# First batch's attention and first weight conversions in a fixed order, with the states requested ahead of the input

## The chip, the cores and the metric

The kernel runs on one core of one Trainium2 chip. The metric is device time in microseconds (us) of one execution; shorter is better. The profile is one execution recorded by the hardware profiler. Engines are named as in the profile: PE is TensorE (PEld its weight loads), DVE is VectorE, ACT is ScalarE, POOL is GpSimd, SP is SyncE, which only issues transfers here. A "q" behind an engine's name is that engine issuing a transfer.

## The reference

Three stages follow one another: an attention of each batch against a small state and back, a product MoE layer, and an eight-expert layer with one expert for each token.

```python
scores = scale * np.matmul(x, state.transpose(0, 1, 3, 2))      # x (8,8,512,64), state (8,8,32,64)
a = np.exp(scores - scores.max(-1, keepdims=True))
a /= a.sum(-1, keepdims=True) + 1e-09
xread = np.matmul(a, state)
# sread: the same with the roles of x and state exchanged
x = concat([xread, sread]) as (4608, 512)
x = (x @ w_a) * (x @ w_b) @ w_out                               # w_a, w_b (512,1536), w_out (1536,512)
# then per token: e = argmax(x @ w_gate), gate * sigmoid * (relu(x @ w1[e]) @ w2[e])
```

## The kernel before, in words

Phase 1 goes batch by batch (`main(b)`, b = 0 to 7). The attention of a batch gives a matrix A. The state, multiplied into the weights w_a and w_b, gives a matrix M for each of six groups of 256 columns (`mprep`). A times M (`s1`, twelve steps f, two products each on PE, line 511) gives the two factors; ACT and DVE multiply them and split the product into a high and a low part (`product` and `split`, lines 490 to 498 and 248 to 250). The split product is multiplied by the split w_out (`s2`, line 524). So M of group g needs w_a and w_b of group g, and the first `s2` needs the first two blocks of w_out.

**Conversions.** The weights are not used as they lie in memory. `converter` is a generator over 18 items, in the order (0,a), (0,b), (1,a), (1,b), w_out 0, (2,a), (2,b), w_out 1 and so on. Each item is loaded in two requests on SP's queue into one of two buffers (the tiles y and yT, not otherwise used so early), goes through two passes on ACT (line 184 writes cr, line 185 writes cx) and three on DVE (line 186 a shift of cx, line 196 a merge that is the last reader of the loaded data, line 199 an add of cr). Items of w_out have one more pass on ACT (line 209, wo_h) and one on DVE (line 210, wo_l). The load of item i + 2 is requested once line 196 of item i has read the buffer.

**The first batch.** The attention of batch 0 is not hidden behind another batch's work. A list, `CFG["pro"]`, gives the order in which its units are written: "stt" turns the state (with a copy of it on POOL first, line 240, since the turned state needs two copies side by side), "x0" to "x3" turn the input in quarters (line 309, copies to SBUF at lines 315 and 317), "sc" the scores (324, copies 336 and 337), "af0", "af1" turn the scores and make the exponentials (346, 351, 352, 355), "an" the sums and the division (377 to 382, one half on DVE, the other on POOL), "ab0", "ab1" turn A back and split it (445, 249, 250), "m" is `mprep` of group 0 (480, 249, 250) and "c" is one conversion. Five conversions stand in this list. The other 13 are placed in `main(0)` by `CFG["conv"]`, a count for each of 24 slots: slot 0 comes behind `s1` of f = 0, and for f from 1 on slot 2f - 1 comes behind `s1` of f and slot 2f behind the `s2` of f - 1 that follows it. The `mprep` of groups 1 to 5 stands in slots 1, 5, 9, 13 and 17 of batch 0.

**What sets the order.** The source is not the order of execution. A scheduler takes the instructions of each engine by their place in the source and its own estimate of when their inputs are ready, so that an instruction may be placed ahead of one that stands before it in the source. Each engine then executes its instructions strictly in the order given.

Of the kernel before, what the change touches and what calls it, by code (L numbers as in the profile page):

```python
# [36 lines left out]
SCALE = 0.125  # L37
BYPE = 2
CFG = {
    "pro": ["c", "stt", "x0", "x3", "x1", "x2", "sc", "c", "af0", "af1", "c", "an", "c", "ab0", "ab1", "m", "c"],  # L40
    "conv": [0, 1, 0, 1, 1, 0, 1, 1, 1, 0, 1, 1, 1, 0, 1, 1, 1, 0, 0, 1, 0, 0, 0, 0],
    "at0": [10, 14, 10, 12, 15, 15, 15, 18, 18, 20, 21, 23, 23, 23],
    "at": [6, 7, 9, 10, 11, 13, 14, 17, 18, 15, 19, 21, 22, 23],
    "gate": [1, 2, 3, 5, 6, 7, 9, 10, 11, 17],
# [7 lines left out]
class Phase1:  # L52
# [30 lines left out]
    def run(self, ctx, moe2):  # L83
# [35 lines left out]
        self.conv = self.converter(order)  # L119
        self.att = u = self.attention(0)  # L120
        conv = lambda n: [next(self.conv, None) for _ in range(n)]
        units = {"m": lambda: self.mprep(0, 0), "c": lambda: conv(1)}
        for n, v in u.items():
            units.update({n + str(i): w for i, w in enumerate(v)} if isinstance(v, list) else {n: v})
        for n in CFG["pro"]:
            units[n]()
        self.banks = cycle([(self.ps_x, "aux")])

        for b in range(self.nb):
# [17 lines left out]
    def converter(self, order):  # L147

        nc = self.nc
        V = nc.vector
        n = 1024
        raws = {}

        def load(i):  # L160
            if i >= len(order):
                return
            it = order[i]
            raw = raws[i] = self.craw[i % 2]
            for k in range(2):
                to = raw[:, n * k : n * k + n]
                if isinstance(it, int):
                    f = 2 * it + k
                    nc.sync.dma_start(out=to, in_=self.w_out[P * f : P * f + P, :])
                else:  # L170
                    g, ab = it
                    src = (self.w_a, self.w_b)[ab][2 * P * k : 2 * P * k + 2 * P, 512 * g : 512 * g + 512]
                    nc.sync.dma_start(
                        out=to.rearrange("p (a b) -> p a b", a=2), in_=src.rearrange("(j p) f -> p j f", p=P)
                    )

        def step(i):
            raw = raws.pop(i)
            it = order[i]
            w = raw.rearrange("p (n two) -> p n two", two=2)  # L180
            lo, hi = w[:, :, 0].bitcast(U32), w[:, :, 1]
            r = self.pc.tile([P, n], U16, tag="cr", name="cr")
            x = self.pc.tile([P, n], I32, tag="cx", name="cx")
            nc.scalar.activation(out=r, in_=lo, func=AF.Copy, scale=2.0**-29)
            nc.scalar.activation(out=x.bitcast(F32), in_=hi.bitcast(F32), func=AF.Copy, scale=2.0**-112)
            V.tensor_scalar(out=x, in0=x, scalar1=3, scalar2=None, op0=ALU.logical_shift_left)
            if isinstance(it, int):
                to, v = x, lambda t: t
                half = x.bitcast(U16).rearrange("p (n two) -> p n two", two=2)[:, :, 0]
            else:  # L190
                g, ab = it
                v = lambda t: t.rearrange("p (j f) -> p j f", j=4)
                to = self.wab[:, ab, :, 256 * g : 256 * g + 256].bitcast(I32)
                half = self.wab.bitcast(U16)[:, ab, :, 512 * g : 512 * g + 512]
                half = half.rearrange("p j (f two) -> p j f two", two=2)[:, :, :, 0]
            V.scalar_tensor_tensor(
                out=to, in0=v(hi), scalar=-(1 << 31), in1=v(x), op0=ALU.bitwise_and, op1=ALU.bitwise_or
            )
            V.tensor_tensor(out=half, in0=half, in1=v(r), op=ALU.add)
            return x.bitcast(F32)  # L200

        for i in range(2):
            load(i)
        for i in range(len(order)):
            v = step(i)
            load(i + 2)
            if isinstance(order[i], int):
                h, l = (t[:, 2 * order[i] : 2 * order[i] + 2, :].rearrange("p f n -> p (f n)") for t in (self.wo_h, self.wo_l))
                nc.scalar.activation(out=h, in_=v, func=AF.Copy)  # L209
                V.tensor_tensor(out=l, in0=v, in1=h.bitcast(F32), op=ALU.subtract)  # L210
            yield
# [10 lines left out]
    def load_x(self, b):  # L222
# [2 lines left out]
        st = self.p2.tile([P, 2, 1 if turned else 2, D], F32, tag="st", name=f"st_{b}")  # L225
        srcs = self.state[b].rearrange("(j q) n d -> q j n d", q=2)
        for q in range(2):
            (nc.scalar if b == 0 else nc.sync).dma_start(out=st[:, q, 0, :], in_=srcs[q])
        if turned:
            xin = self.px.tile([P, 4, 16, 32], F32, tag="xin", name=f"xin_{b}")  # L230
            src = self.x[b].rearrange("(j k) (o i c) (a e) -> k a j i c o e", k=2, i=32, c=4, e=32)
# [4 lines left out]
                        in_=src[g // 2, g % 2, j],  # L236
                    )
            self.at.setdefault(b, {}).update(xin=xin)
        else:
            nc.gpsimd.tensor_copy(out=st[:, :, 1, :], in_=st[:, :, 0, :])  # L240
        t = self.p1.tile([P, H, 4 * D], F32, tag="x", name=f"x_{b}")
        src = self.x[b].rearrange("h (p c) d -> p h (c d)", c=4)
# [13 lines left out]
    def attention(self, b):  # L256
# [116 lines left out]
        def anorm():  # L373
# [3 lines left out]
                nc.vector.tensor_reduce(out=sm[:, g, :], in_=d["A"][:, g, :], axis=AX.X, op=ALU.add)  # L377
            nc.vector.tensor_scalar(out=sm, in0=sm, scalar1=1e-9, scalar2=None, op0=ALU.add)
            nc.vector.reciprocal(out=sm, in_=sm)
            for hf, e in enumerate((nc.vector, nc.gpsimd)):  # L380
                g = slice(16 * hf, 16 * hf + 16)
                e.tensor_tensor(
                    out=d["A"][:, g, :], in0=d["A"][:, g, :], in1=sm[:, g, :].to_broadcast([P, 16, 32]), op=ALU.mult
# [163 lines left out]
    def main(self, b):  # L547
# [25 lines left out]
                put(h, x)  # L573
        if b == 0:
            for h in range(24):
                put(h, *[lambda: next(self.conv, None)] * CFG["conv"][h])
        sl = self.slots(prog, 24)
        ys = None
        gts = {}
# [14 lines left out]
    def main_sr(self):  # L594
# [48 lines left out]
            pass  # L643
        self.acc = ys
        self.evac(self.nb)

    def gate(self, b, T):
        nc, p1, p2 = self.nc, self.p1, self.p2
# [1146 lines left out]
```

## Time and profile before

| | us |
|---|---|
| median of 3 runs (lowest to highest) | 1206.18 (1206.01 to 1207.05) |
| time of the profiled execution | 1205.72 |
| its span, first to last instruction | 1204.1 |
| first main product (`s1` of batch 0, line 511) starts | 36.85 |
| PE busy over the span | 1141.3 (95%) |
| DVE busy over the span | 628.6 (52%) |
| ACT busy over the span | 437.9 (36%) |
| mean granted PE clock, share of full | 0.975 |

The span is the time from the first to the last instruction; the profiled execution took 1.6 us more than its span. Busy shares are means over stages with different limits, so the change is read from the stretch in which it lies.

### The profile page before, as it was taken

What the parts mean: (1) busy time and instruction counts of PE and PEld (TensorE: products, weight loads), DVE (VectorE), ACT (ScalarE), POOL (GpSimd) and SP (SyncE); (2) the same over time, 40 slices, a digit from 0 to 9 for tenths busy, and PEclk for the clock granted to TensorE, in tenths of its full rate; (3) what the DMA queues carried; (4) which work ended last, traced back from release to release, by engine and by line L of the source; (5) the groups of instructions that cost most, each with busy time, mean ns of one, the idle gap of its engine ahead of it and who ended that gap; (6) DMA issues with size and microseconds to landing.
All of it is one profiled execution on the core that took longest, in us unless ns stands there. A gap on an engine that the chain in (4) does not pass through costs nothing. (4 is left out here: it accounts for less than half of the span.)

```text
span 1204.1 us, 19174 instructions
## 1 busy us (share of the span) xinstructions
PE 1141.3 (95%) x7076; PEld 906.3 (75%) x7076; DVE 628.6 (52%) x1078; ACT 437.9 (36%) x720; POOL 178.3 (15%) x282
## 2 busy tenths in 40 slices
PE   3898999999999999999999999789999999999994
PEld 2665767777777677677677789678888998888983
DVE  5889545465464364554643354842443444454462
ACT  4666424333333333333442244431321323242341
POOL 1100002001001020020010101002233123332121
PEclk7899999999999999999999999898999999999997
DMA  6563320302203003010000008539272162635610
GB/s 200 179 226 105 71 38 36 70 4 72 36 1 97 11 36 71 1 52 20 1 36 2 36 1 203 103 108 206 81 198 71 37 164 75 171 89 156 164 33 21
DMA packets 97453, 98.79 MB, mean 82 GB/s; under 512 B 58556, under 2 KB 69853, under 8 KB 97309
## 3 DMA queue, kind: packets, MB, share of 16 engines
q1 hardware_dynamic: 87508, 71.53, 23.3%
q0 software_dynamic: 9536, 25.41, 7.0%
q8 instruction: 74, 1.21, 0.4%
q14 instruction: 71, 0.57, 0.2%
q10 hardware_dynamic: 264, 0.07, 0.0%
HBM read 76.75 MB, written 21.02 MB: 81 GB/s over the span
## 5 line engine op out<-in xcount | busy, mean ns | idle before, releaser
L979 PEld LDWEIGHTS ps_h<-yT,w 128*128 128x128 f32 x1536 | 191.4, 191 | 12.2 <-issue 6.4
L979 PE MATMUL ps_h<-yT,w 128*128 128x256 f32 x1536 | 193.6, 283 | 6.1 <-issue 6.0
L1000 PE MATMUL ps_o<-w,hT 128*128 (+1 forms) x768 | 190.1, 396 | 2.4 <-DVE hT L940 2.4
L524 PE MATMUL ps_y<-wo_h,gh 128*128 128x512 f32 x408 | 165.9, 411 | 2.0 <-ACT wo_h L209 2.0
L1000 PEld LDWEIGHTS ps_o<-w,hT 128*128 128x128 f32 x768 | 139.8, 188 | 32.4 <-issue 3.0
L524 PE MATMUL ps_y<-wo_l,gh 128*128 128x512 f32 x408 | 161.5, 396 | 0.5 <-DVE wo_l L210 0.5
L524 PE MATMUL ps_y<-wo_h,gl 128*128 128x512 f32 x408 | 161.0, 395 | 0.0
L496 DVE TENSOR_TENSOR a<-a,ps_ab 128x512 f32<-128x512 f32 x96 | 65.6, 684 | 156.0 <-PE ps_ab L511 150.7
L511 PE MATMUL ps_ab<-Ah,Mh 128*128 128x512 f32 x384 | 128.3, 415 | 6.0 <-ACT Mh L249 6.0
L511 PE MATMUL ps_ab<-Al,Mh 128*128 128x512 f32 x384 | 121.6, 398 | 0.0
L511 PE MATMUL ps_ab<-Ah,Ml 128*128 128x512 f32 x384 | 120.7, 396 | 0.0
L511 PEld LDWEIGHTS ps_ab<-Ah,Mh 128*128 128x128 f32 x384 | 67.7, 191 | 58.4 <-issue 25.1
L934 ACT ACTIVATE hT<-ps_h 128x512 fp32r<-128x512 f32 x64 | 38.0, 594 | 197.5 <-PE ps_h L979 189.9
L495 ACT ACTIVATE a<-ps_ab 128x512 f32<-128x512 f32 x96 | 57.3, 597 | 118.9 <-PE ps_ab L511 118.9
L940 DVE SCALAR_TENSOR_TENSOR hT<-ps_h,hT 128x512 fp32r<-128x512 f32 x64 | 44.0, 688 | 106.0 <-ACT hT L934 106.0
L524 PEld LDWEIGHTS ps_y<-wo_h,gh 128*128 128x128 f32 x408 | 76.7, 189 | 26.3 <-issue 7.1
L249 ACT ACTIVATE gh<-a 128x512 fp32r<-128x512 f32 (+1 forms) x108 | 65.4, 605 | 83.8 <-DVE a L496 83.5
L250 DVE TENSOR_TENSOR gl<-a,gh 128x512 fp32r<-128x512 f32 (+1 forms) x108 | 71.3, 660 | 41.0 <-ACT gh L249 40.3
L960 POOL DMA_INDIRECT out<-yT,gt x37 | 46.6, 1259 | 301.9 <-DVE yT L950 224.6
L524 PEld LDWEIGHTS ps_y<-wo_h,gl 128*128 128x128 f32 x408 | 76.7, 188 | 18.4 <-DVE gl L250 0.2
L524 PEld LDWEIGHTS ps_y<-wo_l,gh 128*128 128x128 f32 x408 | 77.0, 189 | 15.6 <-DVE wo_l L210 1.0
L250 DVE TENSOR_TENSOR Ml<-ps_m,Mh 128x512 fp32r<-128x512 f32 x96 | 61.8, 686 | 48.3 <-ACT Mh L249 48.2
(245 smaller groups left out, 1398.0 us busy)
## 6 DMA issues: line engine op xcount, KB each, us to landing
raw<-in_moe_w SPq DMA_DIRECT2D x32, 512.0 KB, 10.2
raw<-in_moe_w SPq DMA_DIRECT2D x8, 2048.0 KB, 8.5
x<-in_x SPq DMA_DIRECT2D x7, 1024.0 KB
xin<-in_x SPq DMA_DIRECT2D x96, 64.0 KB
y<-in_moe_w_a SPq DMA_DIRECT2D x8, 512.0 KB
yT<-in_moe_w_b SPq DMA_DIRECT2D x8, 512.0 KB
y<-ysort POOLq DMA_DIRECT2D x28, 128.0 KB, 5.8
y<-in_moe_w_out SPq DMA_DIRECT2D x6, 512.0 KB
```

Of the source, the lines that this page charges most:

```text
L249: self.nc.scalar.activation(out=hi, in_=src, func=AF.Copy)
L250: self.nc.vector.tensor_tensor(out=lo, in0=src, in1=hi.bitcast(F32), op=ALU.subtract)
L495: nc.scalar.activation(out=a[:, 0:n], in_=pa[:, 0:n], func=AF.Copy)
L496: nc.vector.tensor_tensor(out=a[:, 0:n], in0=a[:, 0:n], in1=pb[:, 0:n], op=ALU.mult)
L511: nc.tensor.matmul(out=ps, lhsT=m[:, ab, q, c0 : c0 + P], rhs=r[:, q, :], start=i == 0, stop=i == 5)
L524: nc.tensor.matmul(out=y, lhsT=l[:, sl], rhs=r[:, f, :], start=f == 0 and i == 0, stop=f == NFC - 1 and i == 2)
L934: return e.activation(out=self.hT[:, j % 2, :, 0, :], in_=self.ps_h[j % 2].rearrange("p (f n) -> p f n", f=2), func=AF.Relu)
L940: return e.scalar_tensor_tensor(out=l, in0=self.ps_h[j % 2].rearrange("p (f n) -> p f n", f=2), scalar=0.0, in1=h.bitcast(F32), op0=ALU.ma ...
L960: return e.indirect_dma_start(out=self.out, out_offset=bass.IndirectOffsetOnAxis(ap=to[0:rows].bitcast(U32), axis=0), in_=self.ob[t][0:row ...
L979: m = e.matmul(out=self.ps_h[j % 2][:, G * (f % 2) : G * (f % 2) + G], lhsT=self.w1[:, wh, x : x + P], rhs=self.yT[:, c, yh, :], start=k == 0,
L1000: m = e.matmul(out=self.ps_o[2 * (k % 2) + t], lhsT=self.hT[:, j % 2, f, hh, P * t : P * t + P], rhs=self.w2c(slot, wh, 2 * j + f), start= ...
```

## The change

In the list of the first batch, the attention's units stand first, in their natural order; the first conversion follows the scores; three conversions remain in the list instead of five, and the two others move into `main(0)`, in slots 0 and 1 (item (1,b) and w_out 0). Items (2,a), (2,b) and w_out 1 go from slots 1, 3 and 4 to slots 3, 4 and 5; from slot 6 on the slots hold the same items as before. A conversion is now two units: "ca", its two ACT passes, with cx (line 185 before) written ahead of cr, and "cd", its three DVE passes, the next load and the passes for w_out. `pin` adds an order without any wait between successive instructions of the list on PE, ACT and DVE, so that the scheduler keeps the source's order among them. A unit "warm" runs one tiny ACT instruction at the start. The states of batch 0 are requested twice, on SP's queue ahead of the input and on ACT's queue, each into one of the two places, in place of the copy on POOL. Both halves of the first batch's division are on DVE.

```diff
-    "pro": ["c", "stt", "x0", "x3", "x1", "x2", "sc", "c", "af0", "af1", "c", "an", "c", "ab0", "ab1", "m", "c"],
-    "conv": [0, 1, 0, 1, 1, 0, 1, 1, 1, 0, 1, 1, 1, 0, 1, 1, 1, 0, 0, 1, 0, 0, 0, 0],
+    "pro": "warm stt x0 x1 x2 x3 sc ca af0 af1 cd ca an cd ab0 ab1 m ca cd".split(),
+    "conv": [1, 1, 0, 1, 1, 1, 1, 1, 1, 0, 1, 1, 1, 0, 1, 1, 1, 0, 0, 1, 0, 0, 0, 0],
...
+            "warm": lambda: nc.scalar.activation(out=warm, in_=self.ones[:, 0:1], func=AF.Copy),
...
+        at = self.mark()
         for n in CFG["pro"]:
             units[n]()
+        self.pin(at, nc.tensor, nc.scalar, nc.vector)
...
+            nc.scalar.activation(out=x.bitcast(F32), in_=hi.bitcast(F32), func=AF.Copy, scale=2.0**-112)
             nc.scalar.activation(out=r, in_=lo, func=AF.Copy, scale=2.0**-29)
-            nc.scalar.activation(out=x.bitcast(F32), in_=hi.bitcast(F32), func=AF.Copy, scale=2.0**-112)
+            yield
...
-            (nc.scalar if b == 0 else nc.sync).dma_start(out=st[:, q, 0, :], in_=srcs[q])
+            nc.sync.dma_start(out=st[:, q, 0, :], in_=srcs[q])
+            if b == 0:
+                nc.scalar.dma_start(out=st[:, q, 1, :], in_=srcs[q])
...
-        else:
+        elif b:
             nc.gpsimd.tensor_copy(out=st[:, :, 1, :], in_=st[:, :, 0, :])
...
-            for hf, e in enumerate((nc.vector, nc.gpsimd)):
+            for hf, e in enumerate((nc.vector, nc.gpsimd if b else nc.vector)):
...
-                put(h, *[lambda: next(self.conv, None)] * CFG["conv"][h])
+                put(h, *[lambda: next(self.conv, None)] * (2 * CFG["conv"][h]))
...
+    def mark(self):
+        return len(self.nc.cur_bb.bb.instructions)
+
+    def pin(self, at, *engines):
+
+        last = {}
+        for i in self.nc.cur_bb.bb.instructions[at:]:
+            if i.engine not in [e.engine for e in engines]:
+                continue
+            if i.engine in last:
+                self.tc.add_manual_dep(
+                    i,
+                    last[i.engine].name,
+                    mybir.DependencyInfo(mybir.DependencyClass.NoSync, mybir.DependencyReason.DATA),
+                    reason="in the order of the source",
+                )
+            last[i.engine] = i
```

## Rows read from the trace of the kernel before

**Rows 1.** Stretches: start:end, length, busy us of each engine, PEclk, DMA share, GB/s.
```profile
0.00:36.80 36.80, 14.37 (x84) 7.99 (x84) 23.00 (x31) 17.14 (x21) 8.57 (x26) 0.69 0.63 206
...
36.85:59.00 22.15, 22.13 (x111) 16.19 (x110) 19.04 (x25) 15.00 (x23) 0.00 (x0) 0.89 0.49 153
59.00:125.00 66.00, 57.24 (x382) 40.97 (x383) 61.09 (x79) 42.73 (x59) 2.41 (x2) 0.97 0.47 157
...
155.00:808.00 653.00, 646.90 (x4009) 489.08 (x4008) 335.65 (x702) 234.74 (x431) 63.45 (x124) 0.99 0.19 47
```
**Rows 2.** Waits of PE, whole execution: us in total, times, longest.
```profile
PE ps_ab L445 <- DVE A L382: 7.0, 1, 7.0
PE ps_ab L511 <- ACT Mh L249: 6.0, 4, 2.2
...
PE ps_ab L445 <- POOL A L382: 1.4, 1, 1.4
```
**Rows 3.** Timeline of the first 17 us: start, us, what, [idle before <-releaser].
```profile
0.95 2.00 SPq L245 DMA_DIRECT2D x<-in_x  x4
0.95 1.77 ACTq L228 DMA_DIRECT2D st<-in_state  x2
...
3.86 0.44 PE L309 MATMUL ps_xt<-ident,x 128*128 128x128 f32 x1 [3.86 <-DMA x<-in_x]
...
7.37 0.28 POOL L240 COPY st<-st 128x128 f32<-128x128 f32 x1 [5.76 <-DMA st<-in_state]
...
8.19 3.13 PE L309 MATMUL ps_xt<-ident,x 128*128 128x128 f32 x15
...
9.93 1.28 ACT L184 ACT_TABLE_LOAD   x1 [9.93 <-DMA y<-in_moe_w_a]
...
13.89 2.43 PE L324 MATMUL ps_s<-xT,stT 64*32 64x256 f32 x32 [2.57 <-ACT xT L315]
...
16.63 0.67 DVE L337 COPY sc<-ps_s 128x512 f32<-128x512 f32 x1
```
**Rows 4.** Groups of DVE, first 36.8 us: busy us, mean ns, idle before.
```profile
L199 DVE TENSOR_TENSOR wab<-wab,cr 128x1024 uint16<-128x1024 uint16 x4 | 5.4, 1359 | 0.0
L186 DVE TENSOR_SCALAR cx<-cx 128x1024 int32<-128x1024 int32 x5 | 3.5, 700 | 2.2 <-ACT cx L185 2.2
L196 DVE SCALAR_TENSOR_TENSOR wab<-y,cx 128x1024 int32<-128x1024 int32 x2 | 2.5, 1234 | 0.0
...
L351 DVE TENSOR_REDUCE mx<-ps_af 128x16 f32<-128x512 f32 x2 | 1.4, 696 | 0.7 <-PE ps_af L346 0.7
...
L387 DVE TENSOR_REDUCE m<-sc 128x2 f32<-128x1024 f32 x1 | 1.2, 1237 | 0.0
L382 DVE TENSOR_TENSOR A<-A,sm 128x512 f32<-128x512 f32 x1 | 0.7, 726 | 0.0
```
**Rows 5.** Timeline of PE's `mprep` and the conversions' third load.
```profile
15.40 0.90 SPq L173 DMA_DIRECT2D y<-in_moe_w_a  x2
...
20.72 1.14 ACT L184 ACTIVATE cr<-y 128x1024 uint16<-128x1024 uint32 x1 [3.73 <-DMA y<-in_moe_w_a]
...
22.46 1.96 PE L480 MATMUL ps_m<-wab,stT 64*32 64x512 f32 x16 [3.45 <-DVE wab L199]
```
**Rows 6.** Groups of ACT, first 36.8 us.
```profile
L249 ACT ACTIVATE Mh<-ps_m 128x512 fp32r<-128x512 f32 x2 | 1.1, 586 | 0.0
```
**Rows 7.** Timeline behind the start of `s1`: PE at two clocks, DVE's longest wait.
```profile
39.58 1.06 PE L511 MATMUL ps_ab<-Ah,Mh 128*128 128x512 f32 x2
...
42.18 0.69 DVE L496 TENSOR_TENSOR a<-a,ps_ab 128x512 f32<-128x512 f32 x1 [2.46 <-ACT sc L390]
...
43.27 0.62 PE L511 MATMUL ps_ab<-Ah,Mh 128*128 128x512 f32 x2
```
**Rows 8.** Waits of DVE, 36.8 to 120 us: us in total, times, longest.
```profile
DVE cx L186 <- ACT cx L185: 2.5, 3, 1.2
```
**Rows 9.** A stretch ahead of `s1`, columns as in the first group.
```profile
24.00:36.00 12.00, 3.57 (x18) 1.61 (x10) 10.57 (x16) 6.61 (x9) 3.64 (x1) 0.50 0.60 206
```

More of the change, by code (lines that the diff above doesn't have):

```diff
@@ L121, in run @@
         conv = lambda n: [next(self.conv, None) for _ in range(n)]
-        units = {"m": lambda: self.mprep(0, 0), "c": lambda: conv(1)}
+        warm = self.cpool.tile([P, 1], F32, name="warm")
+        units = {
+            "m": lambda: self.mprep(0, 0),
+            "ca": lambda: conv(1),
+            "cd": lambda: conv(1),
+            "warm": lambda: nc.scalar.activation(out=warm, in_=self.ones[:, 0:1], func=AF.Copy),
+        }
         for n, v in u.items():
             units.update({n + str(i): w for i, w in enumerate(v)} if isinstance(v, list) else {n: v})
+        at = self.mark()
         for n in CFG["pro"]:
             units[n]()
+        self.pin(at, nc.tensor, nc.scalar, nc.vector)
         self.banks = cycle([(self.ps_x, "aux")])
@@ L204, in converter @@
         for i in range(len(order)):
-            v = step(i)
+            v = yield from step(i)
             load(i + 2)
```

## The prediction

> **What bounds the kernel now.** I read the stretches first, then PE's waits, then the first 45 us instruction by instruction, since every edit lies there. Outside the first batch PE sets the time: from 155 to 808 us it is busy for 646.9 of 653 us [rows 1]. What is gained or lost ahead of that is therefore passed on to the end; I found nothing later that is tied to a fixed time.
>
> In the first 36.8 us PE is busy for 14.37 us and DVE for 23.00 [rows 1]: a chain through DMA, ACT and DVE sets the time. The reader is to see in the rows where the attention stands behind a conversion. The state lands at 7.37, and PE had stood since one early transpose at 3.86 [rows 3]. The scores are late because ACT loads its table at 9.93 and runs conversion passes ahead of the turned input (PE waits 2.57) [rows 3]. A is late because DVE weaves four conversions into the softmax: PE waits 7.0 us for the division on DVE and 1.4 more for the half on POOL [rows 2]. The first `s1` starts at 36.85.
>
> Behind that the bound is not PE alone. From 59 to 125 us PE is idle for 66 - 57.24 = 8.76 us while DVE is busy for 61.09 of 66; PE's largest wait there is for M [rows 1, 2], which ends a chain of conversions. So an early `s1` is worth no more than the lead that DVE gets on its conversions. That is the quantity to work out.
>
> **State, table, input.** The copy on POOL goes (it is 0.28 us behind the landing [rows 3]). SP now issues two state requests before the input. The two on ACT's queue took 1.77 us, so I delay the input, and the loads behind it, by 1.77 [rows 3]. When the state lands is not shown for the new order. Lower end: the first input quarter landed 3.86 - 0.95 = 2.91 us after its issue began; the second state request begins half of 1.77 after 0.95, so 1.8 + 2.9 = 4.7. Upper end: 7.3 as now, if its small pieces again wait among those of the input. I take 5.5, nearer to the lower end, since the input's requests now start only when all state requests are out. ACT's two requests end at 2.72 as now; the table load of 1.28 follows them and ends near 4.1. ACT has nothing else until the first turned quarter after 6, so it costs nothing; without this cover it would cost 1.28. The tiny activation behind it goes with it.
>
> Then, in source order: 18 transposes at 3.13/15 = 0.21 us [rows 3] run from 5.5 to 9.3. The last input quarter landed before 8.19 (the 15 transposes ran without a wait), so before 9.96 with the delay; I take 9.5 for the end of the transposes. The last turned quarter leaves through DVE (0.69, like the copy at 16.63), a quarter of the scores follows (2.43/4 = 0.6), and the score copies (0.67): 9.5 + 0.7 + 0.6 + 0.7 = 11.5. Before, this point was 17.3 [rows 3]: **5.8 us earlier**.
>
> **Softmax, two conversions, M.** From here on DVE's order is the source's. Four transposes at twice 0.21, since the clock was at half in this part [rows 9], with their start: 1.0. Two maxima and two subtractions at 0.70: 2.8. Conversion 0: 0.70 + 1.23 + 1.36 = 3.3. The sums twice 0.70, two small steps taken at 0.6, and two halves of the division at 0.73, where before one was on POOL: 3.5. Conversion 1: 3.3 [rows 4]. `mprep` 1.96 [rows 5] and the first Mh 0.59 [rows 6]. The split of A and its transposes fit beside `mprep` and conversion 1. Sum: 1.0 + 2.8 + 3.3 + 3.5 + 3.3 + 2.0 + 0.6 = 16.5. Successive DVE spans overlap: the groups of the first stretch add up to some 25.7 us, of which 23.00 is union over 31 instructions [rows 1], or 0.09 for each; 14 of them give back 1.2. So `s1` starts at 11.5 + 15.3 = 26.8, **10 us earlier**. The ACT passes of conversion 0 need their load, which had landed by 9.93; with 1.77 more it comes at 11.7, just as the scores are out, and ACT has cx ready long before DVE asks at 15.3.
>
> **What of the 10 us is DVE's.** At 36.85 DVE before had done four conversions, the shift of the fifth and the maximum of the second softmax (line 387). In the new order it ends the low part of M at 28.1 (26.8 plus the second Mh and two overlapped subtractions) with two conversions done. It lacks two conversions 6.6, the shift 0.7 and line 387 1.2, and has done half a division more, 0.7 [rows 4]: 7.8, less 0.09 for each of nine overlaps, 7.0. It is level at 35.1: a **lead of 1.7 us**, not 10. The moved conversions bring their loads along. A buffer asked for at 15.40 was used at 20.72 [rows 5], 5.3 us. The load of item 3 is requested after line 196 of conversion 1, near 22.5, and lands near 27.8, in time; that of item 4 after conversion 2, near 30.5, and lands near 35.8. ACT, which works in order, may hold M's copies behind it; DVE has conversion 3 and two products meanwhile. SP has nothing else queued behind them.
>
> On top comes DVE's wait of 2.46 for the first product, ending at 42.18 [rows 7]: with `s1` ten us earlier this product is there when DVE comes. That gives 1.7 + 2.4 = 4.1. Writing cx ahead of cr lets line 186 start one ACT pass sooner; it waited 2.5 in three places from 36.8 to 120 [rows 8], which I bound between 0 and 2.3. Against it stands PE's clock: `s1` starts at half clock as before, and I expect some idle time of PE until w_out 0 is ready, and so another stretch at half clock. I set these two off against each other.
>
> The sum: **4.0 us**. The profiled execution took 1205.72, which gives 1201.7; the median of the runs is 0.5 higher, so I forecast **1202.2**. Its own range is a gain of 2.5 to 6: 1200.2 to 1203.7.
>
> **Rivals.**
>
> *PE's lead is kept* (0.13). If the scheduler fills DVE and ACT well, PE keeps most of its 10 us; at most the 8.76 us of PE's idle time from 59 to 125 shrinks too. For it: ACT is busy for only 42.73 of those 66 us. Against it: DVE is at 93% there [rows 1]. I give it a gain of 6 to 8.8: 1197.4 to 1200.2, in the middle 1198.8.
>
> *The state comes no earlier* (0.23). It lands at 7.3, and the transposes then end 1.8 later; the lead on DVE falls from 1.7 to zero and only the wait of 2.4 is gained, which a little less overlap takes below what can be told. The time would be 1206.2 - 2.2 = 1204.0. For it: the state was asked for at 0.95 already and was the last thing that PE waited for [rows 3]. Against it: it was asked for together with the input then. The Trainium skill (Trainium Kernel Development and Optimization, Key Constraints) says that requests from several queues run on the same DMA engines and interleave, and that issuing from more than one saves only issue time. By that rule the order on the queues buys no landing time except through what is requested earlier, and the input pays its 1.77; the result would be this rival's 1204.0 and not 1202.2. The landing at 7.37 beside the input agrees with interleaving. I call the bound for telling a change of this kernel from none 0.2%, 2.4 us; this rival stands at its edge, and I count it as no change.
>
> *PE falls back to half clock inside the batch, slower* (0.09). Place: between the second `s1` and the first `s2`. Two `s1` steps end near 34; w_out 0, now behind the batch's start, lands near 35.8 and takes an ACT pass, three DVE passes and line 209 before `s2` can start near 41. Seven idle us may take the clock down; with the stretch at 0.50 before `s1` in view [rows 9], that is what idle time did. A pair of products took 1.06 at half clock and 0.62 behind it [rows 7], 0.22 for each. It decides once more than 4.0/0.22 = 18 products of 512 columns run at half clock on PE's path; 36 (two `s2` and an `s1`) cost 7.9, which gives 1206.2 + 3.9 = 1210.1. For it: PE had no idle time from 36.85 to 59 [rows 1], so there each lost us counts. Against it: the clock was back at 43.27 after the first `s1` [rows 7], and DVE's pace hides a part.
>
> **How the numbers follow.** Forecast 0.55, the three rivals 0.13, 0.23 and 0.09. Faster by over 0.2% (below 1203.8): 0.55 + 0.13 = 0.68. Within 0.2%: 0.23. Slower by over 0.2%: 0.09. The range leaves out the far end of the first rival and the last rival: 1198.0 to 1206.5, where the upper end is a lead that is lost wholly.
>
> **What would show each step.** State: POOL's copy gone, the first stt transpose between 4.7 and 7.3. Input: the last turned quarter near 9.5. Scores: the copies end near 11.5. No wait of PE for POOL; `s1` starts near 26.8. Lead of DVE: the products that wait for the second group's M some 4 us earlier than before, and the end of the first batch by as much. The prediction is wrong if the state lands as late as now, if the scheduler weaves later work into the list despite the fixed order, or if DVE or ACT finds new waits for loads after `s1`'s start. It is also wrong if a later stage gives the gain back.

## The result, and the profile after

The changed kernel took 1213.99 us (median of 5 runs, 1211.98 to 1217.94) beside 1207.05 for the kernel before on the same chip: a ratio of 1.0058 [1.0044, 1.0073], about 7 us slower. Forecast were 1202.2 and a range up to 1206.5. The profiled execution took 1213.99, its span 1212.3.

The stretches come first, with the columns of [rows 1]; the last two are new.

```profile
0.00:36.80 36.80, 18.60 (x103) 11.85 (x104) 21.80 (x32) 17.01 (x25) 4.54 (x24) 0.77 0.51 162
36.85:59.00 22.15, 15.01 (x70) 10.51 (x69) 19.84 (x23) 14.24 (x18) 0.00 (x0) 0.77 0.63 205
59.00:125.00 66.00, 57.67 (x378) 40.76 (x378) 59.41 (x77) 42.04 (x56) 1.24 (x2) 0.95 0.50 165
155.00:808.00 653.00, 647.17 (x4006) 488.22 (x4006) 335.71 (x702) 234.23 (x430) 63.70 (x124) 0.99 0.19 48
...
36.00:48.00 12.00, 4.86 (x27) 2.29 (x26) 11.02 (x13) 7.71 (x11) 0.00 (x0) 0.68 0.71 241
```

PE does 4.23 us more in the first 36.8 us (18.60 against 14.37), so the attention is earlier. But between 36.85 and 125 it stands for 7.14 + 8.33 = 15.47 us, where it stood for 0.02 + 8.76 = 8.78 before: 6.69 more. That leaves a net loss of 2.5 us. DVE is busy for 21.80 us in the first stretch instead of 23.00, though it now has half a division more to do. The stretch from 155 to 808 is as before. The places where PE stands are in the view of its waits (whole execution, columns as in [rows 2]):

```profile
PE ps_y L535 <- ACT wo_h L218: 9.5, 3, 3.6
PE ps_ab L456 <- DVE A L393: 9.0, 2, 8.7
PE ps_m L491 <- DVE wab L208: 5.4, 2, 3.5
PE ps_st L276 <- DMA st<-in_state: 5.1, 2, 3.9
PE ps_ab L522 <- ACT Mh L260: 2.1, 2, 1.4
```

The wait for `Mh` fell from 6.0 to 2.1 us, and the one for POOL is gone. The wait for the division is still there, for both halves on DVE now. A wait of 9.5 us for `wo_h` took their place; before it was 2.0:

```profile
PE ps_y L524 <- ACT wo_h L209: 2.0, 2, 1.8
```

PE's own timeline shows where each lies (start, us, what, [idle before <-releaser]):

```profile
3.92 0.45 PE L276 MATMUL ps_st<-ident,st 128*128 128x128 f32 x1 [3.92 <-DMA st<-in_state]
5.53 0.47 PE L276 MATMUL ps_st<-ident,st 128*128 128x128 f32 x1 [1.16 <-DMA st<-in_state]
5.80 1.91 PE L320 MATMUL ps_xt<-ident,x 128*128 128x128 f32 x8
8.78 2.27 PE L320 MATMUL ps_xt<-ident,x 128*128 128x128 f32 x8 [1.06 <-DMA x<-in_x]
10.98 2.47 PE L335 MATMUL ps_s<-xT,stT 64*32 64x256 f32 x32
...
30.66 1.65 PE L522 MATMUL ps_ab<-Ah,Mh 128*128 128x512 f32 x3 [0.72 <-ACT Mh L260]
...
41.30 1.96 PE L491 MATMUL ps_m<-wab,stT 64*32 64x512 f32 x16 [3.54 <-DVE wab L208]
46.87 2.07 PE L535 MATMUL ps_y<-wo_h,gh 128*128 128x512 f32 x4 [3.60 <-ACT wo_h L218]
...
78.44 2.08 PE L535 MATMUL ps_y<-wo_h,gh 128*128 128x512 f32 x4 [2.47 <-ACT wo_h L218]
...
97.17 1.20 PE L535 MATMUL ps_y<-wo_h,gh 128*128 128x512 f32 x4 [3.44 <-ACT wo_h L218]
```

The first `s1` starts at 30.66 instead of 36.85. PE runs two of them, then stands for 3.54 us for the second group's M and, behind that, for 3.60 for w_out 0. In the stretch 36 to 48 the granted clock is 0.68 (before it was 0.77 there, with `s1` beginning at half clock), and the four products at 46.87 take 2.07 us: half clock again, after idle time. On DVE (timeline, same columns) the reader is to see what stands ahead of the first conversion, and when each merge (line 205) comes:

```profile
13.53 0.69 DVE L348 COPY sc<-ps_s 128x512 f32<-128x512 f32 x1 [1.75 <-PE ps_s L335]
14.33 1.22 DVE L398 TENSOR_REDUCE m<-sc 128x2 f32<-128x1024 f32 x1
...
18.83 1.23 DVE L205 SCALAR_TENSOR_TENSOR wab<-y,cx 128x1024 int32<-128x1024 int32 x1
...
25.16 1.23 DVE L205 SCALAR_TENSOR_TENSOR wab<-yT,cx 128x1024 int32<-128x1024 int32 x1
...
32.90 1.23 DVE L205 SCALAR_TENSOR_TENSOR wab<-y,cx 128x1024 int32<-128x1024 int32 x1
...
38.17 1.22 DVE L205 SCALAR_TENSOR_TENSOR wab<-yT,cx 128x1024 int32<-128x1024 int32 x1
...
42.45 1.23 DVE L205 SCALAR_TENSOR_TENSOR cx<-y,cx 128x1024 int32<-128x1024 int32 x1
```

The same on DVE before, where the merge is line 196:

```profile
13.38 0.69 DVE L186 TENSOR_SCALAR cx<-cx 128x1024 int32<-128x1024 int32 x1 [1.91 <-ACT cx L185]
14.11 1.23 DVE L196 SCALAR_TENSOR_TENSOR wab<-y,cx 128x1024 int32<-128x1024 int32 x1
...
19.23 1.21 DVE L196 SCALAR_TENSOR_TENSOR wab<-yT,cx 128x1024 int32<-128x1024 int32 x1
...
25.69 1.24 DVE L196 SCALAR_TENSOR_TENSOR wab<-y,cx 128x1024 int32<-128x1024 int32 x1
...
29.56 1.21 DVE L196 SCALAR_TENSOR_TENSOR wab<-yT,cx 128x1024 int32<-128x1024 int32 x1
...
37.11 1.22 DVE L196 SCALAR_TENSOR_TENSOR cx<-y,cx 128x1024 int32<-128x1024 int32 x1
```

The first five merges end at 20.1, 26.4, 34.1, 39.4 and 43.7 us. Before, they ended at 15.3, 20.4, 26.9, 30.8 and 38.3: items 0 to 4 are 4.7, 6.0, 7.2, 8.6 and 5.4 later. The next load is issued behind each merge, so SP's requests moved too: 20.12 for the third, where [rows 5] have 15.40.

The first batch's end is read from the first copy-out of its output. Before and after (timeline of ACT):

```profile
130.53 0.60 ACT L533 ACTIVATE y<-ps_y 128x512 f32<-128x512 f32 x1 [2.38 <-PE ps_y L524]
```
```profile
134.54 0.60 ACT L544 ACTIVATE y<-ps_y 128x512 f32<-128x512 f32 x1 [2.38 <-PE ps_y L535]
```

It is 4.0 us later. From there to about 740 us the lag stays between 3.9 and 3.6 us, then grows to 8.2 at the end of this execution. So two things are to be explained: 4 us in the first 125, and some more in the expert stage.

### The profile page after: what moved, and what is told of

It is laid out like the page before. It is cut to its first block, busy times and chain, and to the rows that moved or that the text cites. A ratio compares the mean times of both kernels' runs of the same rounds, so it can differ in the third digit from the quotient of the medians.

```text
span 1212.3 us, 19185 instructions
## 1 busy us (share of the span) xinstructions
PE 1144.1 (94%) x7076; PEld 907.8 (75%) x7076; DVE 630.3 (52%) x1079; ACT 438.4 (36%) x721; POOL 173.3 (14%) x280
## 5 line engine op out<-in xcount | busy, mean ns | idle before, releaser
L1008 PEld LDWEIGHTS ps_h<-yT,w 128*128 128x128 f32 x1536 | 194.1, 192 | 12.2 <-issue 6.4
L1008 PE MATMUL ps_h<-yT,w 128*128 128x256 f32 x1536 | 196.6, 284 | 6.1 <-issue 6.0
L522 PEld LDWEIGHTS ps_ab<-Ah,Mh 128*128 128x128 f32 x384 | 68.5, 193 | 54.1 <-issue 25.1
L506 ACT ACTIVATE a<-ps_ab 128x512 f32<-128x512 f32 x96 | 57.3, 597 | 119.2 <-PE ps_ab L522 119.2
```

The costliest lines, as they stand in the source:

```text
L506: nc.scalar.activation(out=a[:, 0:n], in_=pa[:, 0:n], func=AF.Copy)
L522: nc.tensor.matmul(out=ps, lhsT=m[:, ab, q, c0 : c0 + P], rhs=r[:, q, :], start=i == 0, stop=i == 5)
L1008: m = e.matmul(out=self.ps_h[j % 2][:, G * (f % 2) : G * (f % 2) + G], lhsT=self.w1[:, wh, x : x + P], rhs=self.yT[:, c, yh, :], start=k == 0,
```

## The experiments

After the result my theory was this (A in the forecasts below). The order without waits holds conversions back behind the attention on DVE; the chain of conversions, with its loads, is what PE's output steps wait for; so an earlier `s1` buys nothing and late conversions cost. Its rivals: the two conversions that left the list are missed (B); the state requests delay the input; the tiny ACT instruction or its tile costs something (C); PE's own order (two `s1`, then the output step at the head of its queue while w_out 0 is not ready) makes the wait (D).

Every run in one table. `s1` and `s2` are the starts of the first of each; "first batch" is the start of the first copy-out less 130.53; all these come from one profiled execution of each kernel. "Whole" is the median less that of the kernel before on the same chip. The ratio goes by all runs and not by the medians, so where the difference is small its sign can be another (e1). The profiled execution need not be near the median: e1's took 1201.45 us (median 1206.02), g2's 1216.39 (median 1210.47). None of these kernels leaves out part of the computation.

| kernel | s1 | s2 | first batch | whole | ratio [95%] |
|---|---|---|---|---|---|
| before | 36.85 | 45.73 | 0 | | |
| changed | 30.66 | 46.87 | +4.0 | +6.9 | 1.0058 [1.0044, 1.0073] |
| e1_no_pin | 32.49 | 45.40 | -3.0 | -0.5 | 1.0006 [0.9989, 1.0022] |
| e2_five | 30.74 | 46.12 | +0.2 | +1.7 | 1.0021 [1.0004, 1.0037] |
| e3_warm_only | 36.04 | 45.00 | -0.6 | +1.7 | 1.0012 [0.9999, 1.0025] |
| e4_state_only | 38.35 | 46.33 | +0.8 | +2.1 | 1.0019 [1.0002, 1.0036] |
| f1_pin_pe_act | 28.57 | 45.37 | +1.8 | +6.1 | 1.0043 [1.0028, 1.0058] |
| f2_no_tile | 29.50 | 46.94 | +4.4 | +6.3 | 1.0048 [1.0029, 1.0066] |
| f3_no_pin_no_tile | 32.33 | 45.24 | -3.7 | -1.4 | 0.9976 [0.9960, 0.9992] |
| f4_swap | 29.93 | 51.70 | +1.2 | +5.3 | 1.0038 [1.0018, 1.0058] |
| g1_dve_free_swap | 29.02 | 50.49 | +0.1 | +0.8 | 1.0003 [0.9986, 1.0021] |
| g2_pin_pe | 34.36 | 44.34 | +2.7 | +3.6 | 1.0037 [1.0021, 1.0052] |
| g3_early | 33.06 | 45.74 | -0.5 | +1.1 | 1.0014 [0.9994, 1.0035] |
| g4_best_old_state | 30.24 | 44.74 | -4.0 | -3.4 | 0.9972 [0.9958, 0.9985] |
| h1_output_first | 32.59 | 45.24 | -3.8 | -0.3 | 1.0001 [0.9986, 1.0015] |
| h2_before_swap | 36.31 | 48.78 | +0.2 | +1.7 | 1.0010 [0.9995, 1.0025] |
| h3_tile_only | 36.60 | 44.86 | +1.3 | +0.9 | 1.0004 [0.9993, 1.0016] |
| h4_best_five | 30.29 | 40.87 | -1.4 | -1.9 | 0.9983 [0.9967, 0.9999] |

h3 sets the scale: one unused tile more moves the first batch by 1.3 us, so a difference of that size in one trace is not put down to an edit. Two other pairs that differ in the tile alone, the changed kernel and f2, e1 and f3, agree within 0.4 and 0.7.

### One part at a time

**e1_no_pin**: the changed kernel without the order among the list's instructions.

```diff
-        self.pin(at, nc.tensor, nc.scalar, nc.vector)
```

> The changed kernel without the fixed order; everything else stays. Theory A (the conversions come too late: the fixed order keeps DVE idle in the attention and delays conversion 0 by 4.7 us): the scheduler weaves the conversions between the attention's units again, line 196's counterpart for item 0 ends some 3 us earlier than in the changed kernel, and the time falls by 2 to 4 us, to 1209 to 1212. Theory B (it is the moving of two conversions into the batch, whatever the order in the list): the first output step still waits for w_out 0, the time stays within 1.5 us of the changed kernel. Theory C (the loss of some 4 us behind 760 us has a cause of its own, the addresses moved by the tiny tile): unchanged there.

The first batch ends 7.0 us sooner than in the changed kernel and 3.0 sooner than before. DVE's timeline:

```profile
13.94 0.69 DVE L194 TENSOR_SCALAR cx<-cx 128x1024 int32<-128x1024 int32 x1 [4.40 <-ACT cx L191]
14.55 0.68 DVE L327 COPY xT<-ps_xt 128x512 f32<-128x512 f32 x1
15.15 1.21 DVE L204 SCALAR_TENSOR_TENSOR wab<-y,cx 128x1024 int32<-128x1024 int32 x1
...
26.23 1.19 DVE L204 SCALAR_TENSOR_TENSOR wab<-y,cx 128x1024 int32<-128x1024 int32 x1
```

The first conversion is back where DVE has nothing else, ahead of the score copies, and the third merge ends at 27.4, not 34.1. This is against rival B, that the two moved conversions alone cost the time: they are still moved here. `s1` starts 1.8 us later than in the changed kernel, and it doesn't matter. The whole time fell by more than forecast, to that of the kernel before and not below; the part behind the first batch is taken up below.

**e2_five**: the order kept, but five conversions in the list, as before, and the slots of before.

```diff
-    "pro": "warm stt x0 x1 x2 x3 sc ca af0 af1 cd ca an cd ab0 ab1 m ca cd".split(),
+    "pro": "warm stt x0 x1 x2 x3 sc ca af0 af1 cd ca an cd ca ab0 ab1 m cd ca cd ca cd".split(),
-    "conv": [1, 1, 0, 1, 1, 1, 1, 1, 1, 0, 1, 1, 1, 0, 1, 1, 1, 0, 0, 1, 0, 0, 0, 0],
+    "conv": [0, 1, 0, 1, 1, 0, 1, 1, 1, 0, 1, 1, 1, 0, 1, 1, 1, 0, 0, 1, 0, 0, 0, 0],
```

> The changed kernel with five conversions in the list again (in the same fixed order, the two behind M's group 0) and the slots of before. Theory B (moved conversions): the first output step no longer waits long for w_out 0 and the first batch ends within 1 us of before; time 1207 to 1210. Theory A (the fixed order delays all conversions): the first product starts 3 to 6 us later than in the changed kernel because ScalarE and VectorE work on conversions ahead of it, and nothing is won: still 3 to 5 us behind before at the end of the first batch.

+0.2 instead of +4.0. With the order in force, moving two conversions behind the list costs 3.8 us. This is what rival B said, and a miss for theory A. Three of e2's merges, for items 0, 2 and 4:

```profile
18.90 1.22 DVE L205 SCALAR_TENSOR_TENSOR wab<-y,cx 128x1024 int32<-128x1024 int32 x1
...
32.64 1.23 DVE L205 SCALAR_TENSOR_TENSOR wab<-y,cx 128x1024 int32<-128x1024 int32 x1
...
41.10 1.23 DVE L205 SCALAR_TENSOR_TENSOR cx<-y,cx 128x1024 int32<-128x1024 int32 x1
```

The first three merges end at 20.1, 26.4 and 33.9 us, as late as in the changed kernel; items 3 and 4 end at 37.6 and 42.3, 1.8 and 1.4 sooner, and PE's wait for `wo_h` falls from 9.5 to 2.5 us. So a late first conversion is not enough for the loss, and by e1 neither is the move of two: it takes both.

**e3_warm_only** and **e4_state_only**: the kernel before with the tiny ACT instruction alone, and with the new state requests alone.

```diff
...
+        warm = self.cpool.tile([P, 1], F32, name="warm")
...
+            "warm": lambda: nc.scalar.activation(out=warm, in_=self.ones[:, 0:1], func=AF.Copy),
...
```
```diff
-            (nc.scalar if b == 0 else nc.sync).dma_start(out=st[:, q, 0, :], in_=srcs[q])
+            nc.sync.dma_start(out=st[:, q, 0, :], in_=srcs[q])
+            if b == 0:
+                nc.scalar.dma_start(out=st[:, q, 1, :], in_=srcs[q])
...
-        else:
+        elif b:
             nc.gpsimd.tensor_copy(out=st[:, :, 1, :], in_=st[:, :, 0, :])
```

> The kernel before with the tiny ScalarE instruction (and its 128-byte tile) alone. Theory C (the tile moves the addresses of what is allocated behind it and slows the expert stage): 3 to 5 us slower than before, all behind 760 us. Rival (the late loss is scatter of the gathers between executions): within 1.5 us of before; the table load leaves conversion 0's way, which gives at most 1.3 us.

> The kernel before with the state requests of the changed kernel alone. If the input and the first loads, requested 1.56 us later, set the start: first product 0.5 to 1.6 us later, time 0.5 to 2 us slower. If the state was what the attention waited for: first product 0.5 to 2 us earlier, time the same or up to 2 us faster. I lean to the first, since ScalarE turns to conversion 0 ahead of the turned input in this order.

Neither makes 4 us (-0.6 and +0.8), and e3 is a miss for the 3 to 5 us that theory C forecast: its ratio is 1.0012 [0.9999, 1.0025]. e4's PE shows what the requests buy and cost:

```profile
5.80 0.47 PE L267 MATMUL ps_st<-ident,st 128*128 128x128 f32 x1 [1.30 <-DMA st<-in_state]
6.13 1.11 PE L311 MATMUL ps_xt<-ident,x 128*128 128x128 f32 x4
...
9.60 2.82 PE L311 MATMUL ps_xt<-ident,x 128*128 128x128 f32 x12 [2.36 <-DMA x<-in_x]
...
16.23 2.43 PE L326 MATMUL ps_s<-xT,stT 64*32 64x256 f32 x32 [3.81 <-ACT xT L317]
```

The state is there at 5.80, but PE now waits for the input, the transposes end at 12.4 instead of 11.3, and the scores start at 16.23 instead of 13.89 [rows 3], behind an ACT that has conversions first.

### Which engine's order, and the tile

**f1_pin_pe_act**: DVE left free, PE and ACT still in the source's order. **g2_pin_pe**: only PE in order.

```diff
-        self.pin(at, nc.tensor, nc.scalar, nc.vector)
+        self.pin(at, nc.tensor, nc.scalar)
```
```diff
-        self.pin(at, nc.tensor, nc.scalar, nc.vector)
+        self.pin(at, nc.tensor)
```

> The changed kernel with the fixed order on TensorE and ScalarE alone; VectorE's order in the list is the scheduler's again (conversions 0 and 1 are woven between the sums of the softmax, the second batch of small softmax steps goes behind them), while every order behind the list stays the same. Theory A (VectorE's fixed order makes the conversions late, and with them w_out 0 and the second M): the conversions are done 0.5 to 2 us earlier, and the first batch ends 0.5 to 2 us earlier than in the changed kernel. Theory D (it is the order that the scheduler then chooses inside the batch): the first batch ends within 0.5 us of the changed kernel.

> The changed kernel with the fixed order on TensorE alone; ScalarE and VectorE free. If ScalarE's fixed order (its passes of conversion 0 behind the score copy, those of conversion 2 behind the copies of M) adds to the loss: conversions 0 to 2 come 2 to 4 us earlier than in the changed kernel and the first batch ends 4 to 7 us earlier. If ScalarE's order is harmless: the same 2.2 us as with VectorE free.

Freeing DVE gives back 2.2 us (+4.0 to +1.8); the second merge is then 3.2 us sooner (end at 23.2), the third only 2.1 (32.0). g2 is a miss: its merges are as early as in e1 (third at 27.6), yet it stands at +2.7. Its waits, from 28 to 130 us:

```profile
PE ps_ab L456 <- DVE A L393: 8.8, 2, 8.3
PE ps_ab L522 <- ACT Mh L260: 6.6, 4, 2.1
PE ps_y L535 <- ACT wo_h L218: 4.3, 2, 2.8
```

The low part of the second group's M is ready at 47.3 where e1 has 42.8. So early merges alone are not enough; what DVE and ACT do behind them may count too, though no run isolates it.

**f2_no_tile**: the tiny instruction works in place on `ones`, without a tile of its own. **f3_no_pin_no_tile**: e1 and f2 together.

```diff
-        warm = self.cpool.tile([P, 1], F32, name="warm")
...
+            "warm": lambda: nc.scalar.activation(out=self.ones[:, 0:1], in_=self.ones[:, 0:1], func=AF.Copy),
```

> The changed kernel, with the tiny ScalarE instruction writing in place into the block of ones, so that no tile is added and no address moves. Theory C (the 128-byte tile shifts what lies behind it and costs time in the expert stage): the pace of the expert stage's products returns from 2.82 to 2.80 us per 24, and the time from 760 us to the end falls by 1 to 3 us. Rival (scatter of the gathers): the pace and the end stay as they are.

> The changed kernel without the fixed order and without the added tile. The first batch ends some 3 us earlier than before, as without the fixed order alone; if the tile costs something behind 760 us, the time falls to 1202 to 1204, 3 to 4 us faster than before; if not, it stays at 1205 to 1206.5.

f2 stays at +4.4: the tile is no part of the first batch's loss. f3 is the first version that beats the kernel before: 0.9976 [0.9960, 0.9992]. Its stretch 36 to 48 and its wait for w_out 0, against 4.86 us of PE at 0.68 and waits of 3.6 in the changed kernel:

```profile
36.00:48.00 12.00, 10.97 (x58) 7.49 (x59) 12.00 (x17) 9.56 (x15) 0.00 (x0) 1.00 0.52 174
```
```profile
PE ps_y L533 <- ACT wo_h L216: 0.3, 1, 0.3
```

**f4_swap**: in the changed kernel, the first output step is put behind the third `s1` on PE (`last_s1` is the last PE instruction of that step). **g1_dve_free_swap**: f4 with DVE free, as in f1.

```diff
...
+            elif b == 0 and f == 1:
+                pass
             else:
+                if b == 0 and f == 2:
+                    m = self.mark()
+                    self.s2(ys, gts.pop(0), 0)
+                    self.behind(m, last_s1)
+                    next(sl)
...
```

> The changed kernel with the third product step of the first batch (s1 of f = 2) put ahead of the first output step (s2 of f = 0) on TensorE. Theory D (TensorE's order inside the batch is what costs: it stands 3.6 us before w_out 0): the wait for w_out 0 is filled and the first batch ends 2 to 4 us earlier than in the changed kernel. Theory A (the conversions themselves are late): the third product step waits for the second M instead, which is ready 1 us behind w_out 0, and the first batch ends within 1 us of the changed kernel.

> The changed kernel with both partial cures: VectorE free in the list and the third product step ahead of the first output step on TensorE. Alone they brought the end of the first batch 2.2 and 2.7 us forward, of the 7.0 that the kernel without any fixed order has over the changed one. If they are separate causes: some 4.9 us forward, 1 us ahead of before. If both cure the same wait: 2.7 to 3.2 us forward, 1 us behind before.

The swap gives 2.8 us (+1.2), the free DVE 2.2, both 3.9 (+0.1). f4 comes out as theory D forecast, and g1 between its two forecasts: PE's order is worth something while w_out 0 is late. In whole time only g1 is clear of the changed kernel; the intervals of f1 and f4 overlap with its own. The 3 us from here to e1 belong to no single edit that I tried.

### Late conversions or the order as such

**g3_early**: the full order kept, but the three conversions of the list stand earlier in the source; the two others stay moved.

```diff
-    "pro": "warm stt x0 x1 x2 x3 sc ca af0 af1 cd ca an cd ab0 ab1 m ca cd".split(),
+    "pro": "warm stt x0 x1 x2 x3 ca sc cd ca af0 af1 cd ca an cd ab0 ab1 m".split(),
```

> The changed kernel with the fixed order on all three engines, but the conversions earlier in the list: passes of conversion 0 ahead of the scores on ScalarE and directly behind them on VectorE, conversion 1 ahead of the sums, conversion 2 ahead of M. Theory A (it is the conversions' late place, not the fixed order as such): conversions 0 to 2 come 2 to 5 us earlier than in the changed kernel, and the first batch ends at least 3 us earlier, though the first product step starts 1 to 3 us later. If a fixed order as such costs: the first batch ends within 1.5 us of the changed kernel.

-0.5 instead of +4.0, with `s1` at 33.06, 2.4 us later than in the changed kernel. With the conversions early in it, an order of the same kind on the same engines ends the batch about where the kernel before does: the 4 us are not the price of an order as such, but of the place of the conversions in it. The batch still ends 2.5 us later than in e1; whether that is the order or the place that remains is not shown. The whole times of e1, e2 and g3 agree: their intervals end at 1.0022, 1.0037 and 1.0035, below the changed kernel's 1.0044.

The swap in f4 and g1 left one theory open: that the kernels without the order gain because PE runs a third `s1` ahead of the output step (theory D), and not by their conversions.

**h1_output_first**: f3, with the third `s1` put behind the first output step on PE, which takes from f3 what f4 gave to the changed kernel. **h2_before_swap**: f4's swap in the kernel before.

```diff
+                at_s1 = self.mark()
                 gts[f] = self.s1(b, f)
+                if b == 0 and f == 2:
+                    self.behind(at_s1, last_s2)
...
```

> The kernel without fixed order and without the added tile, with the first output step (s2 of f = 0) put ahead of the third product step (s1 of f = 2) on TensorE again, as in the kernel before. Theory D (TensorE running ahead of w_out 0 is what wins): the wait for w_out 0 comes back, and the first batch ends 2 to 5 us later, at most 1.5 us ahead of before. Theory A (the earlier conversions win by themselves): the first batch still ends 3 us or more ahead of before.

> The kernel before, with only the third product step put ahead of the first output step on TensorE. There w_out 0 came before the second M, so theory D alone gives nothing: the first batch ends within 1 us of before. If running ahead is worth something by itself (the output steps then stand behind fewer waits): 1 to 3 us earlier.

h1's PE, waits from 28 to 130 us, and ACT's last pass for `wo_h` and first copy-out:

```profile
PE ps_y L533 <- ACT wo_h L216: 5.1, 1, 5.1
```
```profile
119.13 1.06 ACT L216 ACTIVATE wo_h<-cx 128x1024 fp32r<-128x1024 f32 x1 [2.39 <-DVE m L397]
...
126.70 0.60 ACT L542 ACTIVATE y<-ps_y 128x512 f32<-128x512 f32 x1 [2.27 <-PE ps_y L533]
```

PE stands for 5.1 us for w_out 0, longer than any single wait for `wo_h` in the changed kernel, and the batch still ends 3.8 us sooner than before. So the theory that PE's running ahead carries the gain falls. What h1 shares with f3 is the start of the conversion chain (first merges within 0.5 us of each other, up to item 4's at 41.0 and 40.8) and its end: the sixth and last pass for `wo_h` starts at 119.1 us, f3's at 119.2; before it was 122.7, and in the changed kernel 126.8. That is 7.6 to 7.9 us ahead of the first copy-out in these four, and 6.3 to 8.4 in all 18. In between it is another matter (the fourth pass starts at 86.4 in h1 and 89.4 in f3). So the batch's end moves with the end of the chain; that the chain sets it is argued from this, since PE does not wait for the last pass before or in the changed kernel. h2 agrees: PE's order alone gives nothing before (+0.2).

### Toward the best version, and the late stage

**g4_best_old_state**: f3 with the states as before (ACT's queue and POOL's copy). **h4_best_five**: g4 with e2's list and the slots of before.

```diff
-            nc.sync.dma_start(out=st[:, q, 0, :], in_=srcs[q])
-            if b == 0:
-                nc.scalar.dma_start(out=st[:, q, 1, :], in_=srcs[q])
+            (nc.scalar if b == 0 else nc.sync).dma_start(out=st[:, q, 0, :], in_=srcs[q])
...
```

> The best version so far (no fixed order, no added tile) with the state requested as before, on ScalarE's queue alone and copied on GpSimd, so that input and first loads are requested 1.56 us earlier. The state requests alone ended the first batch 0.84 us later than before; if that holds here too, the first batch ends 0.8 us earlier still, 4.5 us ahead of before. If the earlier state is worth something in this order: up to 1 us later instead.

> The best version (no fixed order, no added tile, state requested as before) with five conversions in the list and the slots of before. If the two moved conversions cost in the batch also without a fixed order: the first batch ends 0.5 to 2 us earlier still. If moving them is what lets TensorE start early: 1 to 3 us later.

g4 is the best: 1203.47 us beside 1206.86, 0.9972 [0.9958, 0.9985], with the first batch 4.0 us shorter. That the old state requests themselves help (-4.0 against -3.7) is too little to tell. h4 shows the sign of an edit turning: without the order, moving two conversions out of the list helps by 2.6 us (-4.0 against -1.4); with it, the same move costs 3.8 (e2). Each is read from one trace; the ratios of g4 and h4, 0.9972 and 0.9983, have intervals that overlap.

**h3_tile_only**: the kernel before with one unused tile of one float (four bytes) for each partition, which the forecasts call 128 bytes.

```diff
+        nc.gpsimd.memset(cp.tile([P, 1], F32, name="warm"), 0.0)
```

> The kernel before with the 128-byte tile, set to zero by GpSimd at the start and never read, without the ScalarE instruction. Theory C (addresses): 2.82 us per 24 products in the expert stage in place of 2.80, the first seven batches 0.3 to 0.4 us shorter in all, together 1 to 1.5 us slower than before. If it was the instruction: pace and time as before.

The chain that ended last shows the expert stage's groups of 24 products (line 979 before). The kernel before, h3, f2 and the changed kernel:

```profile
834.59 2.80 PE ps_h L979 x24
```
```profile
836.42 2.82 PE ps_h L980 x24
```
```profile
840.89 2.80 PE ps_h L1007 x24
```
```profile
839.57 2.82 PE ps_h L1008 x24
```

In the eight kernels without the tile, the kernel before among them, all but one or two of some 44 such groups in each chain take 2.80 or 2.81 us; in the ten kernels with it all but one or two take 2.82 or 2.83. The tiny instruction has no part in it (f2 has it, h3 doesn't). The twelve products behind each group take 2.80 us in all of them, so a group with these twelve takes 5.63 us instead of 5.60. Some 56 such pairs make 1.5 us. The same chains hold a second difference that goes with the tile: their last two waits for a gather (`gt`, near 1020 and 1080 us) take 23.6 to 25.4 us together in the ten kernels with the tile, and 22.3 to 23.4 in the eight without. No run tells why. The whole times show little of either: h3's ratio is 1.0004 and at most 1.0016, some 2 us.

## Why the prediction was wrong

**State, table, input: right, up to the scores.** The second state's transpose started at 5.53 (5.5 forecast), ACT's table was loaded by 4.0, POOL's copy is gone. The input's last transposes ended at 11.05, not 9.5: the last eight waited 1.06 us for the input and took 2.27 us, 0.28 each and not 0.21. Behind them I counted a quarter of the scores (0.6 us), since the rest could run earlier; PE ran all 32 in 2.47 us at the end. The score copies ended at 14.22 instead of 11.5, 2.7 late. The Trainium skill (Trainium Kernel Development and Optimization, Key Constraints) was quoted against this part: requests from several queues interleave on the same engines. e4 agrees in effect: state 1.9 us sooner, input's transposes 1.1 us later, and no gain. The rival by which the state comes no earlier did not happen.

**Softmax, two conversions, M: nearly right.** From the score copies to `s1` I counted 15.3 us; it took 30.66 - 14.22 = 16.4. On DVE the scheduler still wove four instructions of the second softmax (lines 398, 399, 436, 437) into the list, 1.22 us of it in the first of them: the order binds the list's instructions to one another and doesn't keep others out.

**What of the 10 us is DVE's: the step that failed.** I had DVE level at 35.1 us, a lead of 1.7. The list ended 3.8 us later than I counted (M's low part at 31.93, not 28.1): 2.7 of it the late score copies, 1.1 the part behind them. This alone turns 1.7 into -2.1. The trace gives about the same: DVE has four conversions and the shift of the fifth behind it at 42.41, with four steps of `s1` (0.69 + 0.68 + 0.68 + 0.69 us) done that before came later; less these, 39.7 against 36.85, a lag of 2.8. The error is one of kind, too. I compared what DVE had done and not when it could have done it, and I counted all four conversions before as woven into the softmax. But the first ran from 13.4 to 16.7 us, ahead of the first maximum and mostly while PE was at the scores; the new order made DVE wait there (2.65 us for a turned quarter, 1.75 for the scores) and moved this conversion behind two maxima and two subtractions, where DVE is the bound. e1, which puts it back, and g3, which puts it back inside the order, regain 7.0 and 4.5 us. But e2 regains 3.8 with this conversion as late as here, so its late place costs the 4 us only together with the two conversions that left the list; how the loss divides between them is not shown.

**The loads.** I held that they come in time. They did, mostly, but one request follows each merge, so the chain stayed 5 to 9 us late through item 4. w_out 0 could not be ready near 41: its merge ended at 43.7 and its last DVE pass at 45.1, ACT's pass for `wo_h` started at 45.77, behind one of the next item, and the output step began at 46.87.

**The wait of 2.46 on DVE, regained.** It is gone, but other waits took its place (the first product step still waits 0.98 us for PE): up to 59 us DVE is idle for 15.00 + 2.31 = 17.3 us, before for 13.80 + 3.11 = 16.9. It brought nothing to the sum.

**The third rival happened, at its place and with another price.** Between the second `s1` and the first `s2` PE stood for 3.54 and 3.60 us, near the seven forecast, and the clock fell (0.68). I priced it by half clock alone, 7.9 us against a gain of 4.0. By the windows, idle time is the larger part: 6.69 us more idle less 4.23 us of earlier work is 2.5; the remaining 1.5 of the 4.0 fits the lower clock (0.77 against 0.89 from 36.85 to 59): up to the first copy-out PE is busy for 100.86 us against 99.32, with 601 products in either. And the rival left out that later output steps would wait too (2.47 and 3.44).

**What I did not see at all** is the expert stage: I wrote that I found nothing later that is tied to a fixed time, and took the `warm` instruction as free. Its tile goes with 1.5 us more in the products there, and with longer waits for gathers.

**What stays open.** Whole time less first batch is between -0.5 and 4.3 us over the kernels of the table, with a mean of 2.0 in the ten with the tile and 1.5 in the seven others. So the tile doesn't explain the remainder, and some of it may be luck in the one profile of the kernel before; the last two waits for gathers take 25.1 us in the changed kernel's trace and 22.8 in that of the kernel before, and one trace of each does not tell how far they scatter from execution to execution. Nor did I find one edit for the 3 us between g1 and e1: the scheduler orders everything behind the list anew, and g2 shows that this can cost 5.7 us (+2.7 against -3.0) with merges equally early up to item 4.

## What to carry to other kernels

Before an order is forced on an engine that is near its bound, list what now fills its waiting time: work moved out of a hole into the busy part takes its time there, and every load requested behind it moves along. An earlier start of the busiest engine is worth only the lead of what feeds its second and third step. Test a forced order against the free one, and an edit's sign again after each other edit: here the same move of two conversions gained 2.6 us of the first batch without the order and lost 3.8 with it.

## What the runs showed of the hardware

An unused tile of four bytes in each partition, with nothing reading it, made 24 products of the expert stage take 2.82 us instead of 2.80, in each of ten kernels with it and in none of eight without. It moves what is allocated behind it; that addresses are the cause is argued from this, and no other size or place of the tile was tried. The last two waits for gathers took 23.6 to 25.4 us together in the ten, 22.3 to 23.4 in the eight; that too is without a shown cause.
